# Idle products, a removed filler and a shorter load of the first values at the start of a fused attention and mixture-of-experts kernel

## The chip, the core and the metric

The kernel runs on one core of a Trainium2 chip. A core has a matrix engine (TensorE, "PE" in the profile, with its weight loads as "PEld"), three engines for elementwise work (VectorE "DVE", ScalarE "ACT", GpSimd "POOL"), an engine that issues transfers (SyncE "SP") and sixteen DMA engines that all queues share. Data is in DRAM, in the on-chip memory SBUF, or in PSUM, eight banks into which TensorE writes. The metric is the device time of one execution in microseconds.

## The reference

Eight batches of eight heads, 576 positions, 64 numbers a head, and 32 "packed" queries a head. Two attentions follow each other, then a mixture of experts with one expert a row:

```
def sm_attn(qq, kk, vv):
    s = scale * np.matmul(qq, kk.transpose(0, 1, 3, 2))
    s = s - np.max(s, axis=-1, keepdims=True)
    a = np.exp(s)
    a = a / (np.sum(a, axis=-1, keepdims=True) + 1e-09)
    return np.matmul(a, vv)
p_packed = sm_attn(p, k, v)
out = sm_attn(q, p_packed, p_packed)
...
logits = x @ w_gate
e_idx = np.argmax(logits, axis=1)
...
h = np.maximum(x[mask] @ w1[e], 0.0)
ye = h @ w2[e]
out[mask] = gate_w[mask, None] * eom[mask, e, None] * ye
```

`x` is `out` with the heads side by side: 4608 rows of 512 numbers; `w1[e]` is 512 x 1024 and `w2[e]` is 1024 x 512. Everything is float32.

## The kernel before

The work goes batch by batch. For a batch, `encode` computes the first attention: scores of the packed queries `pt` against the keys (`scores`, `by_head`), maximum, exponential, nine transposes of the weights, the product with the values `vt` (`ps_pp`), a scaling to `ppc`, and its transpose `ppT`. From a sum over `ppT` it guesses the batch's expert (`guess`), whose weights `weights` then loads by a register (`w1`, then `w2` through the staging tiles `wst`). `route` computes the second attention's weights (`ps_s2T`, softmax, `a2T`, `ah`, `al`), `values_up` multiplies the packed values with the expert's first layer (`ps_G`), and `ffn` does the rest (`ps_h`, `hT`, `ps_o`). Rows of other experts are left to a small pass and a loop at the end.

The keys and queries arrive transposed, the values as five blocks of 128 positions: 576 positions are four and a half blocks, and the host fills the half block with zeros. For even heads (`g` = 0) the last block's upper 64 partitions are zero, for odd heads (`g` = 1) its lower 64.

Batch 0 is different, since nothing can hide it. Its keys come in two parts of 320 and 256 positions (`PARTS`), and `packed_by_parts` handles them one behind the other: on TensorE the scores of part one, an idle run `keep_warm(5)`, the scores of part two, then the transposes (`turn`, line 257), five for part one and four for part two, then the product with the values. VectorE and ScalarE work between them.

The order of the work is written out by hand. The string `START` lists the pieces up to the first batch's `ffn`: `k`, `v`, `q` load the next block of keys, values or queries (`fetch`, line 184), `Y` goes one step further in `encode` of batch 0 and `y` in that of the next batch, `t` in `route`, `W` in `weights`, `G` in `values_up`, and a digit calls `keep_warm` with it. Each engine does its instructions in this order. `keep_warm(i)` (line 113) issues products of zeros whose result nobody reads: `CFG["warm"][i]` wide bf16 ones with 512 columns, for `i` = 0 before them `CFG["short"]` small ones, for `i` = 1 an fp32 one with 128 columns instead. `START` as it stands first loads keys and values of batch 0 and then, still before any step of `encode`, its queries and the keys and packed queries of batch 1.

Transfers go through SP's queue and, for three of the first ones, through ScalarE's. Each transfer is given one of eight completion counters in turn (`DMAHW0` to `DMAHW7`), and it is issued only when the transfer that had this counter before has landed.

Of the kernel before, what the change touches and what calls it, by code (L numbers as in the profile page):

```python
# [18 lines left out]

P = 128  # L20
BANK = 512
CFG = dict(raw=6, rq=2, pa=4, w1=2, wst=4, w2=6, a1T=2, at=2, row=2, ht=4, ob=4, up="faaf", last=(4, 2, 3), short=32, warm=(2, 1, 0, 2, 1, 1, 2, 2, 4),
           pool=("w1.0", "w1.1", "w1.2", "w1.3", "w2.0", "w2.1", "w2.2", "w2.3", "w3.3", "w4.3", "w5.3", "w6.3", "w7.3",
                 "al0.0.0"))

START = "kkvvqqkkYYY1YYY3Y4YYtYWttttttyYYt6G7GttGtWtvvqqkkvv"
BESIDE = "8:ry 9:yrr 10:yrrrt 11:yr 12:wrr 13:wrqq 14:rkk 15:r "  # L30
REST = "16:xr 17:x 18:r 19:xvv 20:x 22:x 24:x 25:xxw 26:ww 27:w 28:r 30:r 31:rxxgx 32:xg 33:gw 34:ww"
PLANS = ["1:GG 3:GG 4:GG 5:W 6:W 7:WW 8:W 9:tt 10:tWW 11:Wyy 12:yy 13:tt 14:tt 15:yytt 16:tyy 17:ty 19:y 20:y 21:ryyr 22:yyr "
# [9 lines left out]
def tile_packed_attn_then_moe(ctx, tc, qT, kT, v, pT, w_go, w1, w2, kp, out):  # L42


    nc = tc.nc
# [7 lines left out]
    TF = S // P  # L53
    SF = TF * P
    REM = S - SF
# [9 lines left out]

    NA = CFG["pa"]

# [45 lines left out]
    def keep_warm(i):  # L113

        ps = bank("warm", "a" if i == 5 else "f")
        if i == 0:
            for _ in range(CFG["short"]):
                nc.tensor.matmul(ps[:MQ, :MQ], idle[:, :MQ], idle[:, :MQ], start=True, stop=True)
        for _ in range(CFG["warm"][i]):
            if i == 1:  # L120
# [22 lines left out]
    no_row = float(2 * B * S)  # L143
    key_i = sb.tile([P, B * T * Q * E], I32, tag="hT", name="key_i", bufs=CFG["ht"], **WIDE)
    nc.gpsimd.iota(key_i, pattern=[[1, B * T * Q * E]], base=int(big_id), channel_multiplier=0)
# [11 lines left out]
    row = const.tile([P, B, T], F32, name="row")  # L157
# [16 lines left out]
    def eng(what, *at):  # L174
        return nc.gpsimd if what + ".".join(map(str, at)) in CFG["pool"] else nc.vector

# [7 lines left out]
    def fetch(x):  # L184

        queue = queues["kvq".index(x)]
        if not queue:
            return
        x, b, g = key = queue.pop(0)
        tag = "rq" if x == "q" else "raw"  # L190
        bufs = CFG[tag]
        if x == "v":
            t = sb.tile([P, T, NPAIR * D], F32, tag=tag, name="vt", bufs=bufs, **EVEN)
            (nc.scalar if b == 0 and g else nc.sync).dma_start(t, v[b, g])
        else:
            src = (kT if x == "k" else qT)[b, g]
            if b == 0 and x == "k":
                flat = kT[b].rearrange("h p c s -> (h p c s)")
                at = P * NPAIR * PARTS[0]
                src = (flat[at:] if g else flat[:at]).rearrange("(p c s) -> p c s", c=NPAIR, s=PARTS[g])  # L200
            step = NPAIR // 2 if b == 0 else NPAIR
            if key == ("k", 0, 0):
                n = step * PARTS[0]
                both = sb.tile([P, n + NPAIR * NP], F32, tag=tag, name="kp", bufs=bufs, **EVEN)
                nc.sync.dma_start(both, kp)
                rest = sb.tile([P, step, PARTS[0]], F32, tag="wst", name="k", bufs=CFG["wst"], **EVEN)
                nc.scalar.dma_start(rest, src[:, step:])
                loaded["p", b, g] = both[:, n:].rearrange("p (c n) -> p c n", n=NP)
                loaded[key] = [both[:, c * PARTS[0]:(c + 1) * PARTS[0]] for c in range(step)] + [rest[:, c] for c in range(step)]
                return  # L210
            t = sb.tile([P, NPAIR, src.shape[2]], F32, tag=tag, name=x, bufs=bufs, **EVEN)
            for c in range(0, NPAIR, step):
                (nc.scalar if b == 0 and x == "k" and c else nc.sync).dma_start(t[:, c:c + step], src[:, c:c + step])
            if x == "k" and g == 0:
                pt = sb.tile([P, NPAIR, NP], F32, tag="pt", name="pt", bufs=2)
                nc.sync.dma_start(pt, pT[b])
                loaded["p", b, g] = pt
        if key == ("v", 0, 1):
            nc.sync.dma_start(wgo, w_go)
        loaded[key] = t  # L220
# [704 lines left out]
    def place(plan, b):  # L925

        kinds = dict(x=(encode, 2), y=(encode, 1), Y=(encode, 0), r=(route, 1), t=(route, 0), u=(route, -1), w=(weights, 1), W=(weights, 0),
                     g=(values_up, 1), G=(values_up, 0), l=(first_leftover, 0))
        for c in plan:
            if c in kinds:  # L930
                piece(kinds[c][0], b + kinds[c][1])
            elif c == "d":
                store()
            elif c.isdigit():
                keep_warm(int(c))
            else:
                fetch(c)

    by_hand = tc.manual_schedule()
    by_hand.__enter__()  # L940
    place(START[:4], 0)
    nc.scalar.activation(first, blank[:, 0:1], AF.Exp)
    place(START[4:], 0)
    for b in range(B):
# [74 lines left out]
```

## Time and profile before

| | |
|---|---|
| median of 3 runs | 397.39 us (397.05 to 398.21) |
| the profiled execution | 397.26 us, its span 395.7 us |
| TensorE busy | 387.2 us, 98% of the span |
| VectorE, ScalarE, GpSimd busy | 281.3, 182.2 and 38.3 us |
| DMA | 83.59 MB, mean 211 GB/s |

The profile records one execution. The span runs from its first to its last instruction; the execution's own time is 1.56 us longer. Times in the rows are counted from the span's start. A busy share is an average over stages with different limits, so a stretch is read by what its last wait is for. "releaser" is the instruction or transfer whose end let another one start.

### The profile page before, as it was taken

What the parts mean: (1) busy time and instruction counts of PE and PEld (TensorE: products, weight loads), DVE (VectorE), ACT (ScalarE), POOL (GpSimd) and SP (SyncE); (2) the same over time, 40 slices, a digit from 0 to 9 for tenths busy, and PEclk for the clock granted to TensorE, in tenths of its full rate; (3) what the DMA queues carried; (4) which work ended last, traced back from release to release, by engine and by line L of the source; (5) the groups of instructions that cost most, each with busy time, mean ns of one, the idle gap of its engine ahead of it and who ended that gap; (6) DMA issues with size and microseconds to landing.
All of it is one profiled execution on the core that took longest, in us unless ns stands there. A gap on an engine that the chain in (4) does not pass through costs nothing.

```text
span 395.7 us, 9528 instructions
## 1 busy us (share of the span) xinstructions
PE 387.2 (98%) x3663; PEld 315.4 (80%) x3663; DVE 281.3 (71%) x798; ACT 182.2 (46%) x407; POOL 38.3 (10%) x40
## 2 busy tenths in 40 slices
PE   6999999999999999999999999999999999999995
PEld 3478886879779898787979888788887889798984
DVE  3789699688965977478755886659774796848820
ACT  4375537825545354533726237442645345541401
POOL 3000003510153000200002000020002000020010
PEclk9999999999999999999999999999999999999999
DMA  8999359918961399205990099602961059105901
GB/s 292 338 365 418 117 182 413 391 41 297 406 233 38 117 362 414 80 27 196 402 373 29 16 311 408 240 28 102 348 229 36 28 178 368 40 29 169 322 15 53
DMA packets 36541, 83.59 MB, mean 211 GB/s; under 512 B 3598, under 2 KB 16144, under 8 KB 36496
## 3 DMA queue, kind: packets, MB, share of 16 engines
q1 hardware_dynamic: 36032, 81.74, 56.2%
q10 hardware_dynamic: 432, 1.25, 0.8%
q8 instruction: 29, 0.48, 0.5%
q14 instruction: 16, 0.13, 0.1%
q0 software_dynamic: 32, 0.00, 0.0%
HBM read 67.76 MB, written 15.27 MB: 210 GB/s over the span
## 4 chain that ended last, share of the span: by engine, by line
PE 95%; DMA 4%; SPq 0%; DVE 0%; ACT 0%; issue 0%
PE ps_o L712 45%; PE ps_h L85 26%; PE ps_o L734 8%; PE ps_G L92 4%; PE ps_pp L92 2%; PE ps_s L92 2%; PE ps_s2T L92 2%; DMA vt<-in_v_dram 2%; DMA pt<-in_pT_dram 2%; PE ps_a1T L340 2%; PE ps_lg L92 1%; PE ps_h L662 1%; PE warm L124 1%; PE ps_lo L840 0%; PE ps_lh L840 0%; PE ps_ppT L375 0%
## 5 line engine op out<-in xcount | busy, mean ns | idle before, releaser
L712 PE MATMUL ps_o<-w2h,hT 128*128 128x512 f32 x512 | 165.2, 395 | 0.0
L712 PEld LDWEIGHTS ps_o<-w2h,hT 128*128 128x128 f32 x512 | 96.4, 188 | 23.0 <-issue 1.3
L712 PE MATMUL ps_o<-w2l,hT 128*128 128x512 f32 x256 | 99.9, 390 | 0.0
L681 DVE SCALAR_TENSOR_TENSOR hT<-ps_h,hT 128x256 fp32r<-128x256 f32 x192 | 60.8, 351 | 48.8 <-ACT hT L678 48.0
L85 PE MATMUL ps_h<-ah,Gh 128*128 128x320 f32 (+1 forms) x252 | 76.5, 304 | 0.0
L85 PE MATMUL ps_h<-ah,Gl 128*128 128x320 f32 (+1 forms) x252 | 74.6, 296 | 0.0
L85 PE MATMUL ps_h<-al,Gh 128*128 128x320 f32 (+1 forms) x252 | 74.5, 296 | 0.0
L678 ACT ACTIVATE hT<-ps_h 128x320 fp32r<-128x320 f32 (+1 forms) x128 | 51.5, 414 | 41.1 <-PE ps_h L85 38.8
L597 POOL TENSOR_TENSOR w2l<-wst,w2h 128x1024 fp32r<-128x1024 f32 x13 | 31.8, 2445 | 296.3 <-ACT w2h L594 266.0
L712 PEld LDWEIGHTS ps_o<-w2l,hT 128*128 128x128 f32 x256 | 48.1, 188 | 9.1
L85 PEld LDWEIGHTS ps_h<-ah,Gh 128*128 128x128 f32 x252 | 47.8, 190 | 3.3 <-issue 0.9
L85 PEld LDWEIGHTS ps_h<-al,Gh 128*128 128x128 f32 x252 | 47.8, 190 | 0.4
L85 PEld LDWEIGHTS ps_h<-ah,Gl 128*128 128x128 f32 x252 | 47.8, 190 | 0.0
L594 ACT CAST w2h<-wst 128x1024 fp32r<-128x1024 f32 (+1 forms) x33 | 33.4, 1054 | 0.6 <-PE ps_o L712 0.6
L698 ACT ACTIVATE ob<-ps_o,scm_all 128x512 f32<-128x512 f32 x27 | 18.6, 688 | 31.9 <-PE ps_o L712 27.3
L466 ACT ACTIVATE s<-s 128x576 f32<-128x576 f32 (+2 forms) x18 | 11.4, 633 | 34.3 <-DVE s L463 34.3
L597 DVE TENSOR_TENSOR w2l<-wst,w2h 128x1024 fp32r<-128x1024 f32 (+1 forms) x20 | 23.4, 1168 | 4.9 <-ACT w2h L594 4.8
L77 DVE TENSOR_TENSOR Gl<-ps_G,Gh 128x512 fp32r<-128x512 f32 x28 | 17.4, 682 | 12.9 <-ACT Gh L76 12.9
L734 PE MATMUL ps_o<-w2h,hT 128*128 128x512 f32 x64 | 25.7, 401 | 0.0
L734 PE MATMUL ps_o<-w2l,hT 128*128 128x512 f32 x64 | 25.0, 391 | 0.0
L486 ACT CAST ah<-a2T 128x576 fp32r<-128x576 f32 (+2 forms) x17 | 10.7, 638 | 26.5 <-DVE a2T L478 26.5
L92 PE MATMUL ps_G<-w,ppT 64*32 64x512 f32 (+1 forms) x288 | 16.4, 550 | 0.0
(219 smaller groups left out, 429.2 us busy)
## 6 DMA issues: line engine op xcount, KB each, us to landing
w<-in_w_dram SPq DMA_DIRECT2D x36, 512.0 KB, 5.1
wst<-in_w_dram SPq DMA_DIRECT2D x36, 512.0 KB, 8.6
vt<-in_v_dram SPq DMA_DIRECT2D x15, 640.0 KB, 9.0
k<-in_kT_dram SPq DMA_DIRECT2D x14, 576.0 KB, 10.0
q<-in_qT_dram SPq DMA_DIRECT2D x14, 576.0 KB, 10.4
out_dram<-ob SPq DMA_DIRECT2D x31, 256.0 KB, 3.7
a_d<-a2T SPq DMA_DIRECT2D x16, 320.0 KB, 7.8
q<-in_qT_dram SPq DMA_DIRECT2D x4, 288.0 KB, 6.1
```

The source lines that it names most:

```text
L77: (lo_eng or nc.vector).tensor_tensor(lo, src, f(hi), ALU.subtract)
L85: res = nc.tensor.matmul(dst, a, m, start=j == 0, stop=j == len(seq) - 1)
L92: res = nc.tensor.matmul(dst, a, m, start=j == 0, stop=j == len(seqs[0]) - 1)
L466: nc.scalar.activation(sf[g], sf[g], AF.Exp, scale=QK)
L486: nc.scalar.copy(ah[:, g, ts], a2T[:, g, ts])
L594: nc.scalar.copy(h, x)
L597: eng("w", b, j).tensor_tensor(l, x, f(h), ALU.subtract)
L678: nc.scalar.activation(hT[:, :n], ps, AF.Relu)
L681: nc.vector.scalar_tensor_tensor(hT[:, d0:d0 + s1 - s0], ps[:, s0:s1], 0.0, f(hT[:, s0:s1]), op0=ALU.max, op1=ALU.subtract)
L698: nc.scalar.activation(ob, ob if b < 2 and t_ < 2 else ps, AF.Copy, scale=sc)
L712: nc.tensor.matmul(ps, a, m, start=fc == i == 0, stop=fc == FC - 1 and i == 2)
L734: nc.tensor.matmul(ps, a, m, start=i == 0, stop=i == len(seq) - 1)
```

## The change

Three numbers of the configuration, one character of `START`, and the load of the first batch's values:

- `short` goes from 32 to 24; `warm[0]` from 2 to 8: the products of zeros at the program's start. `warm[5]` goes from 1 to 2: those between the two parts of the first scores.
- The digit `1` behind the third `Y` is gone: one fp32 idle product among the nine transposes.
- The values of batch 0 are loaded in two transfers for each half of the heads: the four full blocks for all 128 partitions, and the last block for the 64 partitions that are not zero. VectorE fills the other 64 with zeros. Later batches load as before.

```
-CFG = dict(... short=32, warm=(2, 1, 0, 2, 1, 1, 2, 2, 4),
+CFG = dict(... short=24, warm=(8, 1, 0, 2, 1, 2, 2, 2, 4),
...
-START = "kkvvqqkkYYY1YYY3Y4YYtYWttttttyYYt6G7GttGtWtvvqqkkvv"
+START = "kkvvqqkkYYYYYY3Y4YYtYWttttttyYYt6G7GttGtWtvvqqkkvv"
...
-            (nc.scalar if b == 0 and g else nc.sync).dma_start(t, v[b, g])
+            queue = nc.scalar if b == 0 and g else nc.sync
+            if b:
+                queue.dma_start(t, v[b, g])
+            else:
+                full, none = (slice(REM, P), slice(0, REM)) if g else (slice(0, REM), slice(REM, P))
+                nc.vector.memset(t[none, TF], 0.0)
+                queue.dma_start(t[:, :TF], v[b, g][:, :TF])
+                queue.dma_start(t[full, TF], v[b, g][full, TF])
```

How this stands on the engines is seen at two places. The first is SP's queue from the first values on (`kp` and an early key block go before them); `vt` are values, `wgo` the weights of the router, `q` and `k` queries and keys, `pt` the packed queries of batch 1, and the bracket names the counter that a transfer waits for. Before:

```order
L194 DMA vt<-in_v_dram 128x1280
L219 DMA wgo<-in_w_go_dram 128x64
L213 DMA q<-in_qT_dram 128x576
L213 DMA q<-in_qT_dram 128x576 [waits DMAHW0_49]
L213 DMA q<-in_qT_dram 128x576 [waits DMAHW1_49]
L213 DMA q<-in_qT_dram 128x576 [waits DMAHW2_49]
L213 DMA k<-in_kT_dram 128x1152 [waits DMAHW3_49]
L216 DMA pt<-in_pT_dram 128x128 [waits DMAHW4_49]
L213 DMA k<-in_kT_dram 128x1152 [waits DMAHW5_49]
```

The same stretch of SP's queue in the changed kernel, with its own line numbers:

```order
L200 DMA vt<-in_v_dram 128x1024
L201 DMA vt<-in_v_dram 64x256
L226 DMA wgo<-in_w_go_dram 128x64 [waits DMAHW0_49]
L220 DMA q<-in_qT_dram 128x576 [waits DMAHW1_49]
L220 DMA q<-in_qT_dram 128x576 [waits DMAHW2_49]
L220 DMA q<-in_qT_dram 128x576 [waits DMAHW3_49]
L220 DMA q<-in_qT_dram 128x576 [waits DMAHW4_49]
L220 DMA k<-in_kT_dram 128x1152 [waits DMAHW5_49]
L223 DMA pt<-in_pT_dram 128x128 [waits DMAHW6_49]
L220 DMA k<-in_kT_dram 128x1152 [waits DMAHW7_49]
```

The order is the same with one transfer more, and ScalarE's queue has one more too, so from `wgo` on each transfer waits for another counter.

The second place is TensorE around the transposes of batch 0, line 257 (`ps_a1T`), between the scores of part two (`ps_s`) and the products with the values (`ps_pp`). Before:

```order
L92 MATMUL ps_s_196<-k,kp 32x256
L92 MATMUL ps_s_197<-k,kp 32x256
L257 MATMUL ps_a1T<-ident,a_206 128x128 x5
L122 MATMUL warm<-blank 128x128
L257 MATMUL ps_a1T<-ident,a_206 128x128 x4
L92 MATMUL ps_pp<-vt,a1T 32x64 x20
```

The same place in the changed kernel:

```order
L92 MATMUL ps_s_199<-k,kp 32x256
L92 MATMUL ps_s_200<-k,kp 32x256
L264 MATMUL ps_a1T<-ident,a_209 128x128 x9
L92 MATMUL ps_pp<-vt,a1T 32x64 x20
L92 MATMUL ps_pp<-vt,a1r 32x64 x4
```

The idle product of line 122 no longer stands between the transposes. Behind this place TensorE's instructions and their order are the same in both kernels, and so are those of GpSimd; VectorE has the two fills more.

## Rows read from the trace of the kernel before

**Rows 1.** The page: span, TensorE's busy time, shares of the chain by engine

```profile
span 395.7 us, 9528 instructions
PE 387.2 (98%) x3663; PEld 315.4 (80%) x3663; DVE 281.3 (71%) x798; ACT 182.2 (46%) x407; POOL 38.3 (10%) x40
...
PE 95%; DMA 4%; SPq 0%; DVE 0%; ACT 0%; issue 0%
```

**Rows 2.** Chain that ended last, first 17 us: start us, us, what

```profile
1.84 7.63 DMA vt<-in_v_dram
9.48 6.49 DMA pt<-in_pT_dram
...
16.11 0.90 PE ps_s L92 x15
```

**Rows 3.** Timeline of TensorE: start us, us, instruction, count, idle before and releaser

```profile
1.24 1.03 PE L118 MATMUL warm<-blank 128*32 128x32 bf16 x32 [1.24 <-DVE blank L106]
2.21 1.03 PE L124 MATMUL warm<-blank 128*128 128x512 bf16 x2
5.38 0.76 PE L92 MATMUL ps_s<-kp 64*32 64x320 f32 x4 [2.14 <-DVE kp L236]
...
9.33 0.63 PE L122 MATMUL warm<-blank 128*128 128x128 f32 x2
9.75 1.06 PE L257 MATMUL ps_a1T<-ident,a 128*128 128x128 f32 x4
...
14.99 0.38 PE L407 MATMUL ps_cs<-one,ones 1*128 1x1 f32 x2
16.11 0.90 PE L92 MATMUL ps_s<-k,pt 64*32 64x288 f32 x16 [0.73 <-DMA pt<-in_pT_dram]
...
19.14 0.66 PE L92 MATMUL ps_G<-w,ppT 64*32 64x256 f32 x16
```

**Rows 4.** Windows: stretch, length, busy by engine, PEclk, DMA share, GB/s

```profile
7.00:8.00 1.00, 1.00 (x17) 0.23 (x16) 0.68 (x2) 0.69 (x3) 0.00 (x0) 1.00 1.00 420
...
14.00:15.00 1.00, 1.00 (x33) 0.36 (x26) 0.83 (x5) 0.00 (x0) 0.00 (x0) 1.00 0.96 387
15.00:16.00 1.00, 0.37 (x10) 0.28 (x2) 0.96 (x4) 0.59 (x3) 0.00 (x0) 1.00 0.29 84
```

**Rows 5.** Groups by form from 7.1, 8.2, 19.1 and 39.6 us: busy us, mean ns

```profile
L92 PE MATMUL ps_s<-k,kp 64*32 64x256 f32 x16 | 1.1, 630 | 0.0
...
L257 PE MATMUL ps_a1T<-ident,a 128*128 128x128 f32 x5 | 1.3, 432 | 0.0
...
L92 PE MATMUL ps_G<-w,ppT 64*32 64x256 f32 x16 | 0.7, 388 | 0.0
...
L340 PE MATMUL ps_a1T<-ident,a 128*128 128x128 f32 x8 | 1.0, 272 | 0.0
```

**Rows 6.** DMA issues at 0.92, 9.86 and 15.12 us: KB, us to landing

```profile
k<-in_kT_dram ACTq DMA_DIRECT2D x1, 320.0 KB, 4.4
...
k<-in_kT_dram SPq DMA_DIRECT2D x1, 576.0 KB, 7.4
...
w<-in_w_dram SPq DMA_DIRECT2D x1, 512.0 KB, 3.5
```

**Rows 7.** Instruction queue from 13.5 to 13.7 us, and whole run: packets, MB, share

```profile
q8 instruction: 1, 0.02, 30.8%
...
q8 instruction: 29, 0.48, 0.5%
```

**Rows 8.** SP's longest wait for values; timeline of SP, VectorE and ScalarE

```profile
SPq L216 <- DMA vt<-in_v_dram: 1.6, 1, 1.6
...
1.84 0.44 SPq L194 DMA_DIRECT2D vt<-in_v_dram  x1
5.09 0.23 DVE L236 TENSOR_SCALAR kp<-kp 128x128 f32<-128x128 f32 x1 [2.88 <-DMA kp<-in_kp_dram]
7.31 0.53 ACT L250 ACTIVATE a<-ps_s,nm 128x320 f32<-128x320 f32 x1 [2.33 <-DVE nm L253]
```

More of the change, by code (lines that the diff above doesn't have):

```diff
@@ L21 @@
 BANK = 512
-CFG = dict(raw=6, rq=2, pa=4, w1=2, wst=4, w2=6, a1T=2, at=2, row=2, ht=4, ob=4, up="faaf", last=(4, 2, 3), short=32, warm=(2, 1, 0, 2, 1, 1, 2, 2, 4),
+CFG = dict(raw=6, rq=2, pa=4, w1=2, wst=4, w2=6, a1T=2, at=2, row=2, ht=4, ob=4, up="faaf", last=(4, 2, 3), short=24, warm=(8, 1, 0, 2, 1, 2, 2, 2, 4),
            pool=("w1.0", "w1.1", "w1.2", "w1.3", "w2.0", "w2.1", "w2.2", "w2.3", "w3.3", "w4.3", "w5.3", "w6.3", "w7.3",
                  "al0.0.0"))
-START = "kkvvqqkkYYY1YYY3Y4YYtYWttttttyYYt6G7GttGtWtvvqqkkvv"
+START = "kkvvqqkkYYYYYY3Y4YYtYWttttttyYYt6G7GttGtWtvvqqkkvv"
 BESIDE = "8:ry 9:yrr 10:yrrrt 11:yr 12:wrr 13:wrqq 14:rkk 15:r "
```

## The prediction

> **What bounds the kernel now.** I read the page's totals first, then the chain of waits, and then only the first 20 us, because every edit lies there. TensorE is busy 387.2 us of a span of 395.7 us and is 95% of the chain that ended last; the DMA has 4% [rows 1]. That 4% is one piece: the chain starts with the first batch's values (issued 1.84, landed 9.47), goes on with the load of the second batch's packed queries, `pt` (issued 9.48, landed 15.97), and from 16.11 to the end it is TensorE [rows 2]. So whatever moves the start of the second batch's scores at 16.11 moves the end one for one, and whatever only makes TensorE reach that place sooner buys idle time in front of it.
>
> The timeline of TensorE shows that place [rows 3]. After idle products that end at 3.24 it has nothing until the first scores at 5.38. It then works through batch 0 up to the small product of line 407 (14.99, last one over at 15.37), and then stands 0.73 us until `pt` lands. Only at 16.11 do the second batch's scores start.
>
> TensorE is slow until about 11 us. [...] It had been idle for 2.1 us just before 5.38 and nearly without a break at work before the rise.
>
> Why does `pt`, 64 KB, take 6.49 us to land? Because SP's queue serves in order, and `pt` stands behind nine earlier transfers on it. The second half of the second batch's keys, next in that queue, was issued at 9.86 and took 7.4 us [rows 6]: it landed at 17.26. The DMA engines move 387 GB/s in 14 to 15 us but only 84 GB/s in 15 to 16, at a share of 0.29 [rows 4]. So most of the sixteen engines had run dry about a microsecond before `pt` had landed: a late remnant held it. At 13.6 us one packet of the instruction queue q8, 0.02 MB, passes on the same engines; the run has 29 of these, 0.48 MB [rows 7]. I take that packet for the cause of the late remnant.
>
> **The change, part by part.**
>
> *Idle products before the first keys* (8 short ones fewer, 6 wide ones more). The 32 short ones last from 1.24 to about 2.21, 0.030 us each; two wide ones end 1.03 us after 2.21, so a slow one follows the other by about 0.43 us [rows 3]. Now 24 short ones end at about 1.96 and 8 wide ones at 1.96 + 8 x 0.43 = 5.4 us, against a first score at 5.38. Nothing is lost in front of the keys, or at most 0.2 us. What it gives is an earlier rise of the clock.
>
> *Between the two parts of the first scores* stands one wide idle product more (0.43 us slow, less than half of that fast), *among the nine transposes* the fp32 idle product goes, which takes the time from 9.33 to 9.75 [rows 3], 0.42 us.
>
> With a fast clock from before 7 us the road to line 407 shortens as follows. Sixteen scores of part two: 1.1 us busy against 0.7 for a group of the same shape [rows 5], 0.45 saved, and everything on VectorE and ScalarE behind them moves up by as much. The last four transposes, 1.06 us for four against 1.0 us for eight [rows 3, 5]: 0.5 saved. The products with the values: about 0.15 by estimate, since they turn fast half way. Sum 1.1 us; the removed idle product lies beside a wait for ScalarE's exponentials, so I do not add it. Line 407 would be over at 15.37 - 1.1 = 14.3 us.
>
> *None of these 1.1 us reaches the end unless `pt` comes sooner too.* It is late next, and its wait then grows from 0.73 to about 1.6 us.
>
> *The values without their zero rows.* Each of the two loads drops 64 KB, 131 kB in all. At the 420 GB/s of 7 to 8 us [rows 4] that is 0.31 us less in front of `pt`. No row shows how fast rows of 1 KB move (half a tile's partitions now get one such row, in a transfer of its own). The bounds are 0 (the 64 small rows take as long as the bytes they replace) and 0.31. I take 0.25, near the upper end, because q and k, with shorter rows than the values, are moved at about the same rate in 14 to 15 us, 387 GB/s.
>
> [...]
>
> *Two more transfers on SP's and ScalarE's queues.* Each costs an issue of about 0.45 us (0.44 for the values on SP) [rows 8]. On ScalarE it pushes the table load and the conversion of the keys; ScalarE then stands 2.33 us before its first exponential, which hides it. The two fills of zeros on VectorE lie in its 2.88 us before the scaling of the packed queries [rows 8]. Without that cover each would cost its own length. On SP a transfer waits for the landing of the one eight places earlier, and two more places shift who waits for whom: the router's weights no longer go at once but when an early key block has landed (0.92 + 4.4 = 5.3 us [rows 6]), the last query block waits for values instead of keys, and `pt` is released by ScalarE's values instead of SP's. Before, `pt` waited 1.6 us there [rows 8]. Now the last query block and the second batch's keys are issued after the values at about 9.2, and `pt` at about 10.1 instead of 9.48. I cost this at nothing, because the queue holds more than 800 KB then, 2 us of work at 0.42 MB per us, and the DMA is busy without a break to 15 us. If that cover were gone, it would cost the 0.6 us by which `pt` is issued later.
>
> *Weights of the first layer.* Their first block is issued at 15.12 and lands 3.5 us later, at 18.6 [rows 6]; its product starts at 19.14 [rows 3]. Issued at about 14.0 it lands no later than now, so it does not bound.
>
> Sum: the second batch's scores start 0.25 us sooner, at 15.86, and TensorE's road to the end is unchanged. The profiled execution took 397.26 us (span 395.7, 1.56 outside), 0.13 under the median of the runs, 397.39. Forecast: 397.26 - 0.25 = **397.0 us**. The clock's phase and small waits behind 16 us may shift it: its own range is 396.5 to 397.5.
>
> **Rivals.**
>
> *A. The late remnant goes away.* If `pt` landed with the rest of its queue, what follows it, 576 KB, would still need 1.4 us up to the emptying at 15.1, so `pt` would have been moved by 13.7 and landed around 14, before TensorE is ready for it at 14.3. Then the whole 1.1 us reach the end: 397.26 - 1.1 = 396.2. For it: TensorE's instruction packet comes at another moment of the queue. Against it: TensorE gets to the same instruction earlier, not later, so the packet still goes before `pt`, and an engine that has to carry it is as late afterwards. [...]
>
> *B. The clock falls back.* TensorE now waits about 1.6 us before the second batch's scores instead of 0.73. [...] Two groups of scores and a group of line 92's G products would cost about 0.45 more each [rows 5], eight wide idle products 8 x 0.2 = 1.6: together 3.0 us, **400.0 us**, slower. For it: before 5.38 there was a gap of 2.1 us and the work after it was slow [rows 3]. Against it: that clock had not been fast before, and the 0.73 us gap left it fast (388 ns afterwards). [...]
>
> *C. `pt` needs its 6.49 us from its issue.* Issued 0.6 us later, it lands 0.6 later: 397.26 + 0.6 = 397.9. For it: the chain names its issue. Against it: the transfer's time is that of a queue in front of it.
>
> **How the numbers follow.** Forecast 0.62, A 0.16, C 0.13, B 0.07, 0.02 for none of these. No change here means within 0.3% of 397.39, that is 396.2 to 398.6, about what a measurement can tell. Faster: more than half of A and a little of the forecast, 0.12. Slower: B and a trace of C, 0.08. The rest 0.80. The range reaches to A's time and over C's: 396.1 to 398.0; it leaves out B and a part of A.
>
> **What would show it.** Right: products of 64x256 at about 390 ns at 7 us, line 407 over by 14.5, a wait for `pt` of 1.3 to 2 us, and scores of batch 1 at 15.7 to 16.0. The first step is wrong if those products still take 630 ns. The second is wrong if `pt` lands before 15 (A) or after 16.3 (C). B shows as products of 600 ns after 16 us. The forecast falls if the scores of batch 1 start sooner by more than 0.8 us or the road behind 16 us changes its length.

## The result, and the profile after

The changed kernel took 399.74 us (median of 5 runs, 398.42 to 400.05) against 397.25 for the kernel before on the same chip: ratio 1.0053, 95% interval 1.0042 to 1.0065. It is slower, by about 2.1 us by the ratio and 2.5 by the two medians; the forecast was 397.0 in a range up to 398.0. Run once more beside other kernels it took 398.85 against 397.34, ratio 1.0042 (1.0028 to 1.0056).

The page of the changed kernel, its span, TensorE's busy time and the chain by engine, against [rows 1]:

```profile
span 398.2 us, 9526 instructions
...
PE 389.5 (98%) x3660; PEld 314.8 (79%) x3660; DVE 281.9 (71%) x800; ACT 182.3 (46%) x407; POOL 38.2 (10%) x40
...
PE 95%; DMA 3%; ACTq 0%; SPq 0%; DVE 0%; issue 0%; ACT 0%
```

2.5 us more of span, and TensorE busy 2.3 us longer with three products fewer. That sum does not locate the loss: the wide idle products at the start alone take 3.59 us instead of 1.03, in time in which TensorE stood before. The timeline of TensorE shows where, to be laid beside [rows 3]:

```profile
1.99 3.59 PE L124 MATMUL warm<-blank 128*128 128x512 bf16 x8
5.75 0.71 PE L92 MATMUL ps_s<-kp 64*32 64x320 f32 x4 [0.16 <-DVE kp L243]
...
14.09 0.38 PE L414 MATMUL ps_cs<-one,ones 1*128 1x1 f32 x2
16.30 1.08 PE L92 MATMUL ps_s<-k,pt 64*32 64x288 f32 x16 [1.83 <-DMA pt<-in_pT_dram]
17.30 1.89 PE L124 MATMUL warm<-blank 128*128 128x512 bf16 x4
...
20.71 0.66 PE L92 MATMUL ps_G<-w,ppT 64*32 64x256 f32 x16
```

Line 407 (now 414) is over at 14.47 instead of 15.37, the wait for `pt` has grown from 0.73 to 1.83, and the second batch's scores start at 16.30 instead of 16.11. Up to here it is the forecast, short of 0.4 us. Behind it four wide idle products take 1.89 us and the first G product starts at 20.71 instead of 19.14. The by-form group at 7.2 us and the windows (stretch, length, busy by engine, PEclk, DMA share, GB/s) say what the clock did, against [rows 4, 5]:

```profile
L92 PE MATMUL ps_s<-k,kp 64*32 64x256 f32 x16 | 0.7, 388 | 0.0
```

```profile
15.00:16.00 1.00, 0.00 (x0) 0.00 (x0) 0.96 (x3) 0.76 (x4) 0.00 (x0) 1.00 1.13 317
16.00:17.00 1.00, 0.70 (x16) 0.21 (x16) 0.84 (x3) 0.42 (x1) 0.00 (x0) 0.76 0.98 225
17.00:18.00 1.00, 1.00 (x10) 0.28 (x3) 0.86 (x4) 0.54 (x2) 0.00 (x0) 0.50 0.73 270
...
20.00:21.00 1.00, 1.00 (x41) 0.43 (x26) 0.00 (x0) 0.53 (x3) 0.00 (x0) 1.00 1.03 414
```

The 64x256 products take 388 ns at 7 us instead of 630: TensorE is fast that early, at a granted clock (PEclk) that reads 1.00 from 7 to 8 us in both kernels. Then, behind the wait for `pt`, the granted clock falls to 0.50, where it stays until about 20 us, and the 64x288 products take 598 and 622 ns, 412 and 415 before. That is rival B, and it was my first theory of the loss. It did not hold: of the five runs, one had a mean granted clock of 1.000, so no such fall, and took 399.52 us.

Where the 2.5 us of this trace lie: 1.57 up to the first G product, 0.32 from there to the last output's issue (394.42 against 392.53), and 0.6 behind that issue, where no work is left. Nearly all of the 0.32 comes at one place: around 234 us ScalarE starts an activation 0.28 us later behind the same product, and everything behind it is late by as much. ScalarE in the kernel before, then in the changed one:

```profile
233.98 0.44 ACT L678 ACTIVATE hT<-ps_h 128x320 fp32r<-128x320 f32 x1 [0.85 <-PE ps_h L85]
```

```profile
235.83 0.98 ACT L685 ACTIVATE hT<-ps_h 128x320 fp32r<-128x320 f32 x2 [1.13 <-PE ps_h L85]
```

All eight traces of kernels with one transfer more on ScalarE's queue show the wait of 1.12 to 1.14, the ten others 0.85 to 0.87. Why is not shown.

The chain, against [rows 2], goes the same way as before, from the values to `pt`, and then to TensorE:

```profile
1.85 7.74 DMA vt<-in_v_dram
...
10.46 5.70 DMA pt<-in_pT_dram
16.16 0.14 issue
16.30 1.08 PE ps_s L92 x16
17.37 1.82 PE warm L124 x4
```

It passes over SP's queue, and that is where the change sits. SP's waits up to 17 us (waited for, us, times, longest), against [rows 8], and its timeline (start us, us, issues):

```profile
SPq L226 <- DMA k<-in_kT_dram: 2.6, 1, 2.6
SPq L220 <- DMA vt<-in_v_dram: 1.8, 1, 1.8
```

```profile
2.32 0.74 SPq L201 DMA_DIRECT2D vt<-in_v_dram  x1
5.62 0.33 SPq L226 DMA_DIRECT2D wgo<-in_w_go_dram  x1
6.00 3.94 SPq L220 DMA_DIRECT2D q<-in_qT_dram  x4
9.98 0.43 SPq L220 DMA_DIRECT2D k<-in_kT_dram  x1
10.46 0.43 SPq L223 DMA_DIRECT2D pt<-in_pT_dram  x1
```

Before, the four query blocks went from 3.08 to 7.38 and the keys at 7.42. Now the router's weights wait 2.6 us for a key block, the last query block 1.8 for values; it is through at 9.94, and the keys follow. The first weights, issued at 14.22 (KB, us to landing, against [rows 6]):

```profile
w<-in_w_dram SPq DMA_DIRECT2D x1, 512.0 KB, 5.5
```

### The profile page after: what moved, and what is told of

The parts are those of the page before. It is cut to its first block, busy times and chain, and to the rows that moved or that the text cites. A ratio compares the mean times of both kernels' runs of the same rounds, so it can differ in the third digit from the quotient of the medians.

```text
span 398.2 us, 9526 instructions
## 1 busy us (share of the span) xinstructions
PE 389.5 (98%) x3660; PEld 314.8 (79%) x3660; DVE 281.9 (71%) x800; ACT 182.3 (46%) x407; POOL 38.2 (10%) x40
## 4 chain that ended last, share of the span: by engine, by line
PE 95%; DMA 3%; ACTq 0%; SPq 0%; DVE 0%; issue 0%; ACT 0%
PE ps_o L719 45%; PE ps_h L85 26%; PE ps_o L741 7%; PE ps_G L92 4%; PE ps_s L92 2%; PE ps_pp L92 2%; DMA vt<-in_v_dram 2%; PE ps_s2T L92 2%; PE ps_a1T L347 2%; DMA pt<-in_pT_dram 1%; PE ps_lg L92 1%; PE warm L124 1%; PE ps_h L669 1%; PE ps_lh L847 0%; PE ps_lo L847 0%; PE ps_ppT L382 0%
## 5 line engine op out<-in xcount | busy, mean ns | idle before, releaser
L705 ACT ACTIVATE ob<-ps_o,scm_all 128x512 f32<-128x512 f32 x27 | 18.6, 688 | 31.7 <-PE ps_o L719 27.2
```

The lines of the kernel that those rows point to most:

```text
L705: nc.scalar.activation(ob, ob if b < 2 and t_ < 2 else ps, AF.Copy, scale=sc)
```

## The experiments

Each was timed in five rounds beside the kernel before (397.25 to 397.85 in different sittings); the ratio to it counts.

**The split load alone** (the edit of `fetch` put into the kernel before).

> The kernel before with the split load of the first batch's values alone (two more transfers). Theory T (the clock falls in the long wait for pt, about 1.4 us; the two extra transfers lengthen the end of the program by 0.6): TensorE reaches line 407 no sooner than before, its wait for pt is about 0.9, no fall; the second batch's scores start 0.2 later at 16.3, the end of the program grows by 0.6: 397.3 + 0.8 = 398.1. Rival R (the extra transfers themselves cause the loss, the slow products are only a sign of late data): 399.5 or more, with slow products after 16 us. Rival N (the longer end is unrelated to the transfers): 397.5.

1.0055 (1.0028 to 1.0082), 2.2 us slower, the whole loss and no fall of the clock: PEclk is 1.00 throughout. The timeline of TensorE:

```profile
15.93 0.99 PE L92 MATMUL ps_s<-k,pt 64*32 64x288 f32 x16 [0.65 <-DMA pt<-in_pT_dram]
...
20.90 0.67 PE L92 MATMUL ps_G<-w,ppT 64*32 64x256 f32 x16 [1.78 <-DMA w<-in_w_dram]
```

`pt` is even earlier than before; what is late is the first weights, 5.7 us from issue to landing against 3.5 [rows 6]. Theory T is wrong for this kernel; R's time is met, without the slow products that it named.

**The idle edits alone** (the changed kernel with the old load of the values).

> The kernel before with the edits of the idle products alone, the values loaded as before. Theory T: pt lands at about 16.0 as before, line 407 is over about 1 us sooner, the wait of 1.6 to 1.8 makes the clock fall, products of 64x256 take about 600 ns after 16 us, 1.4 us lost there and nothing at the program's end: 398.7. Rival R: no slow products, 397.3. Rival N: the end of the program is longer here as well, 399.3.

0.9979 (0.9970 to 0.9988), 0.8 us faster. TensorE:

```profile
14.61 0.72 PE L92 MATMUL ps_s<-k,pt 64*32 64x288 f32 x16 [0.31 <-DMA pt<-in_pT_dram]
...
18.30 0.67 PE L92 MATMUL ps_G<-w,ppT 64*32 64x256 f32 x16 [0.22 <-DMA w<-in_w_dram]
```

In this trace `pt` has landed by 14.6 and the weights, asked for 1.07 us sooner (14.05), land at 18.2. Theory T is wrong here too: no long wait and no fall. The two halves of the change multiply to 0.9979 x 1.0055 = 1.0034, and 1.0053 and 1.0042 were measured for both: the loss needs nothing more than the split load.

**The gap filled** (eight wide idle products between line 414 and the scores of batch 1).

```
-START = "...YYtYWttttttyYYt6G7..."    warm=(8, 1, 0, ...)
+START = "...YYtYWtttttt2yYYt6G7..."   warm=(8, 1, 8, ...)
...
-ps = bank("warm", "a" if i == 5 else "f")
+ps = bank("warm", "a" if i in (2, 5) else "f")
```

> The changed kernel with eight wide idle products between line 414 and the second batch's scores (8 x 0.22 = 1.75 us of the 1.83 it waited for pt). Theory T: TensorE hardly stands, the granted clock stays 1.00, the scores start at 16.2 to 16.3 as in the changed kernel, line 669 comes 1.4 sooner; the longer end stays: 399.7 - 1.4 = 398.3. Rival R: the products after 16 us stay slow or late, 399.7. If eight are too many: the scores start later than 16.4 and 398.5 comes out.

1.0033 (1.0020 to 1.0046); the clock stays at 1.00, the scores start at 16.76 although `pt` landed at 15.6: too many products here, and 1.3 us of loss are left without any fall. The first weights were in time in this trace (14.14 + 4.2 = 18.3); the loss is made of 0.47 at the first G product, which follows the late scores (19.61), 0.34 behind it and 0.6 at the end.

**As many transfers as before** (queries of batch 0 whole, in the changed kernel).

```
-step = NPAIR // 2 if b == 0 else NPAIR
+step = NPAIR // 2 if b == 0 and x == "k" else NPAIR
```

> The changed kernel with the first batch's queries in one transfer for each half instead of two, so that the program has as many transfers as before the change. Theory T: the wait for pt and the fall stay about as they are, but the end of the program is 0.6 shorter: 399.1, the time from the last output's issue to the end of the span back from 3.7 us to 3.1. Rival N: the end stays 3.7, 399.7. Rival R (the number of transfers decides the whole loss): 397.5.

0.9981 (0.9967 to 0.9995): this one edit gives back nearly everything, the start and the end; theory R. In the same sitting the median is 397.18, that of the idle edits alone 396.88, and the 0.28 us around 234 us are still in its trace. `pt` was waited for 1.21 us, and the clock did not fall.

**The packet of the instruction queue** (60 instructions fewer in front: `short=0`, `warm[0]=4` in the kernel before).

> The kernel before with the 32 short idle products in front replaced by two wide ones: the same time on TensorE, 60 instructions fewer. Theory F (the 16 KB packet of TensorE's instruction queue, at 13.60 in the kernel before, holds one DMA engine back, and pt with it): the packet passes after 15 us, pt lands at 14.1 to 14.6 on all engines instead of 15.97, TensorE does not wait for it behind line 407 (over at 15.4), the scores of batch 1 start at 15.4 to 15.6: 397.8 - 0.6 = 397.2, or 397.5 if the first weights, landing at 18.6, take most of it back. Rival L (the late engine has nothing to do with that packet): pt lands at 16.0 as before, 397.8.

1.0002 (0.9992 to 1.0011). TensorE:

```profile
14.84 0.72 PE L92 MATMUL ps_s<-k,pt 64*32 64x288 f32 x16
...
18.55 0.67 PE L92 MATMUL ps_G<-w,ppT 64*32 64x256 f32 x16 [0.22 <-DMA w<-in_w_dram]
```

The packet (0.48 MB in 29 of them [rows 7], so 16.6 KB for one) passed at 14.42, later than the 13.60 of the kernel before and not after 15, the scores start 1.27 us sooner with no wait for `pt`, the first G product 0.59, and the time is the same. The 0.59 last until about 70 us: there ScalarE waits for an output tile that is still being stored, 2.27 us instead of 1.55, and starts later than before (69.91 against 69.81):

```profile
69.91 0.69 ACT L698 ACTIVATE ob<-ps_o,scm_all 128x512 f32<-128x512 f32 x1 [2.27 <-DMA out_dram<-ob]
```

So a `pt` that lands on time is worth little. The same edit with 44 instructions, on the idle edits alone:

> The idle edits alone (values whole), with the 24 short idle products replaced by two wide ones, 44 instructions fewer, the same time on TensorE. Theory F: the packet of the instruction queue passes later than the 13.31 of the run with the idle edits alone, pt lands at 14.5 or sooner, and the load of the first weights bounds from 18.2: 396.9 or up to 0.2 less. If the packet now falls among the keys that stand before pt, one engine is late again: pt at 15.5 to 16, 397.5. Rival L: as the idle edits alone, 396.9, whatever the packet does.

0.9991 (0.9982 to 1.0000); the packet passed at 13.38, `pt` was waited for 1.47 us, and the first G product still came at 18.56. With 60 instructions fewer on the split load alone:

> The split load with the 32 short idle products in front replaced by two wide ones, 60 instructions fewer. Theory F (with the keys issued later the packet of the instruction queue gets in front of them): the packet passes after 13.5, pt lands at 14.8 or sooner, the first weights by 19.0; the end stays 0.6 longer: 398.0. Rival: the slow stretch of the DMA between 13 and 15 us (253 to 319 GB/s in the kernels with the split load, 391 to 407 without) comes from the transfers alone: 1.5 to 2.2 over before as with the split load alone.

1.0054 (1.0034 to 1.0074), the loss unchanged, first G product at 20.92. Theory F is ruled out as its cause. Nor does the packet's moment decide when `pt` lands: with two transfers behind `pt` (below) it passed at 13.60, as in the kernel before, and `pt` landed at 14.9 and not at 15.97. None of these three times shows a cost of the packet, against my reading of [rows 4, 7].

**The end of the program** (kernel before, one late output stored in three pieces).

> The kernel before with one output tile of the fifth batch (256 KB, around 240 us) stored in three transfers instead of one: two transfers more, none of them near the start. Theory C (two more transfers shift which completion counter the last transfer has, and the engines wait for the counters one by one at the end): the first 230 us are unchanged, from the last transfer's issue to the end of the span 3.7 us instead of 3.1: 397.8 + 0.6 = 398.4. Rival N (the longer end of the kernels with the split load came from something else): 397.8.

1.0014 (1.0005 to 1.0023). Its timeline of SP, span and last issue, and that of the kernel before:

```profile
core 0 of [0], span 396.5 us
...
392.68 0.33 SPq L723 DMA_DIRECT2D out_dram<-right  x1
```

```profile
core 0 of [0], span 395.7 us
...
392.53 0.33 SPq L721 DMA_DIRECT2D out_dram<-right  x1
```

3.8 us behind the last issue instead of 3.2, and only 0.15 up to it: theory C holds. It is 3.8 in the changed kernel as well. SP's waits for the counters at the end, one behind another, show the mechanism. In the kernel before, three were left when the last transfer had landed (394.24); in the changed kernel (396.13), as here, nine:

```profile
L954 SPq EVENT_SEMAPHORE  x3: 27/28/28, 394.2 to 394.4; - x3
```

```profile
L961 SPq EVENT_SEMAPHORE  x9: 28/28/28, 396.1 to 396.6; - x9
```

The other engines have three and nine of these waits left as well. The last one through, the queue of TensorE's weight loads (51 ns a wait), is at its branch behind them at 394.6 and at 397.1, 0.4 and 1.0 us after the landing: the 0.6.

The first 230 us of this program are those of the kernel before, so it gives a second trace of them. Here `pt` landed at 14.8 instead of 15.97, TensorE did not wait for it, and the first G product came no sooner (19.27 against 19.14):

```profile
15.51 0.70 PE L92 MATMUL ps_s<-k,pt 64*32 64x288 f32 x13
...
19.27 0.66 PE L92 MATMUL ps_G<-w,ppT 64*32 64x256 f32 x16
```

The late `pt` of [rows 2] belongs to that one execution.

**The changed kernel again.**

> The changed kernel once more, unchanged, for a second trace of it. Theory T (the fall of the clock is what it loses after 16 us): the granted clock falls again between 16 and 20, products of 64x256 take about 600 ns. Theory W (the loss is a late landing of pt or of the first weights, and the fall only one form of it): clock 1.00 throughout and the same 399.7, with the first G product at 20.5 or later because it waits for its weights.

The clock stayed at 1.00 in this trace, behind a wait of 1.43 us, and the kernel was still slower (1.0042). TensorE:

```profile
15.78 0.72 PE L92 MATMUL ps_s<-k,pt 64*32 64x288 f32 x16 [1.43 <-DMA pt<-in_pT_dram]
...
19.67 0.67 PE L92 MATMUL ps_G<-w,ppT 64*32 64x256 f32 x16 [0.97 <-DMA w<-in_w_dram]
```

The scores start at 15.78, sooner than before, and the weights are late: theory W, if at 19.67 and not at 20.5. In the first trace, too, the weights landed only at 19.7 (14.22 + 5.5), so the fall cost there about 1.0 us, from 19.7 to 20.71, and not the 1.4 that I had charged to it.

**Two useless transfers of 32 bytes** in the place of the split.

```
+if x == "v" and b == 0:
+    tiny = const.tile([1, 8], F32, name=f"tiny{g}")
+    (nc.scalar if g else nc.sync).dma_start(tiny, v[b, g][:1, TF, :8])
```

> The kernel before, values loaded whole, with two more transfers of 32 bytes each that nothing uses, one behind the values on SP's queue and one on ScalarE's, where the split load has its own. Theory O (the order: two more transfers make SP issue the last query block, the keys and pt later, at 9.6 to 10.5 instead of 7.0 to 9.5): the start is lost as with the split load alone, the first weights land at 19.5 or later, plus 0.6 at the end: 1.0 to 2.0 over before, 398.6 to 399.5. Theory S (the shape: rows of 1 KB on half the partitions): the start is that of before, only the end is longer: 0.6 over before, 398.1.

1.0063 (1.0043 to 1.0083), as much as the split load. Neither the bytes nor the rows of 1 KB are needed for the loss; two more transfers at these places are enough. SP's timeline and the window from 11 to 15 us:

```profile
6.39 3.95 SPq L213 DMA_DIRECT2D q<-in_qT_dram  x4
10.43 0.39 SPq L213 DMA_DIRECT2D k<-in_kT_dram  x1
```

```profile
11.00:15.00 4.00, 3.71 (x127) 2.34 (x126) 2.21 (x12) 0.64 (x2) 0.42 (x2) 1.00 0.94 299
```

The kernel before moves 412 GB/s there:

```profile
11.00:15.00 4.00, 3.84 (x127) 2.28 (x119) 1.97 (x11) 0.49 (x2) 0.00 (x0) 1.00 1.04 412
```

**The split load with whole queries, without the idle edits.**

> The split load alone with the first batch's queries in one transfer for each half: as many transfers as before the change, and SP issues the keys at about 7.6 again. Theory O: neither the start nor the end loses, within 0.3 of before, and the DMA engines move 380 to 400 GB/s from 13 to 15 us. Theory S: the start loses 1.0 to 1.5 as in the run with the split load alone, 398.5 or more.

1.0006 (0.9998 to 1.0015). Theory O holds, and no gain from the saved 131 kB can be seen. Two more transfers of the values, one of them on ScalarE's queue, with an early last query block therefore lose nothing at the start. Its profiled run was far from the median (400.83 against 397.88): SP took 3.46 us for the four issues of the first weights, 1.94 in the kernel before, and they landed late. Only the DMA's rate before that, 400 GB/s, and the clock (below) are used of it.

**Which issue counts.** One tiny transfer, on SP alone:

> The kernel before with one transfer of 32 bytes more on SP's queue behind the values, none on ScalarE's. SP issues the query blocks as before (the last at about 7.3), the keys only when the values have landed (9.5 instead of 7.4), pt at about 10. Theory K (the late issue of the keys loses the time): the DMA engines move under 330 GB/s from 13 to 15 us, the first weights land at 19.5 or later, 1.0 to 1.6 over before. Theory Q (the late last query block is needed too): as before, within 0.3. The end of the program is not longer: the last transfer has the next counter but one.

1.0012 (1.0003 to 1.0020). Keys and `pt` go nearly as late as in the changed kernel (9.60 against 9.98 and 9.71), the last query block 1.4 us sooner or more, and the rate stays:

```profile
5.72 2.52 SPq L213 DMA_DIRECT2D q<-in_qT_dram  x4
9.60 0.33 SPq L213 DMA_DIRECT2D k<-in_kT_dram  x1
10.07 0.33 SPq L216 DMA_DIRECT2D pt<-in_pT_dram  x1
```

```profile
11.00:15.00 4.00, 3.83 (x127) 2.27 (x119) 2.33 (x13) 0.58 (x2) 0.23 (x1) 1.00 1.04 403
```

Theory K falls; the ratio is a loss of 0.5 us all the same, more than theory Q's 0.3. Two behind `pt` and the keys:

> The kernel before with two transfers of 32 bytes more on SP's queue behind pt and the second batch's keys. Nothing in front of them is issued later, the counters at the end are shifted by two. Theory O (order in front of the keys): the start is as before, the end 0.6 longer: 0.5 to 0.7 over before. Rival (any two transfers more near the start desynchronise the engines): 1.5 to 2.3 over before, as with two in front.

1.0021 (1.0012 to 1.0029): the end alone, since the last output is issued at 392.39, before the 392.53 of the kernel before. Two between the last query block and the keys:

> The kernel before with two transfers of 32 bytes more on SP's queue between the last query block and the second batch's keys. SP issues the last query block as before (7.0 to 7.8), the keys, pt and the second half of the keys as late as with the split load or later (9.9 to 11.2). Theory Q (the cover: with the last query block already queued 3 us of work cover the later issues): DMA rate 390 or more from 11 to 14 us, first weights by 18.7, only the end 0.6 longer: 0.5 to 0.8 over before. Rival P (two transfers anywhere in front of pt): 305 to 320 GB/s, first weights at 19.5 or later, 1.5 to 2.5 over before.

1.0037 (1.0013 to 1.0060), a wide interval because of one run at 401.5; the median is 0.8 over before. SP's timeline and the window:

```profile
3.23 3.55 SPq L217 DMA_DIRECT2D q<-in_qT_dram  x4
10.06 0.36 SPq L217 DMA_DIRECT2D k<-in_kT_dram  x1
```

```profile
11.00:15.00 4.00, 3.72 (x116) 2.16 (x104) 2.31 (x12) 0.34 (x2) 0.13 (x1) 1.00 1.05 397
```

Keys later than in the changed kernel, the first weights at 18.6, and nothing lost at the start, as theory Q had it. Over the kernels that have a trace (end of the last query block's issue, from SP's timeline, and rate from 11 to 15 us, from the windows):

| last query block issued by | kernels | GB/s, 11 to 15 us |
|---|---|---|
| 6.2 to 8.2 us | the twelve others: before, both kernels of the idle edits, all with whole queries, tiny transfers elsewhere or one alone, two late pieces, `pt` behind the keys, fewer instructions | 397 to 416 |
| 9.7 to 10.0 | changed (twice), gap filled | 346 to 365 |
| 10.3 to 10.5 | split alone, two tiny, split with fewer instructions | 299 to 316 |

A late last query block and a low rate go together in all eighteen traces. Every kernel with a late block also has a transfer more on ScalarE's queue; that transfer alone is not the cause, since the two kernels with it and with whole queries keep 403 and 400 GB/s, but a late block without it was not run.

**A long wait at the fast clock** (idle edits alone, `pt` loaded behind the second half of the keys).

> The idle edits alone (values whole), with pt loaded behind the second half of the second batch's keys instead of in front of it: TensorE, fast since about 6 us, waits for pt from 14.2 to about 16.9, 2.6 us. Theory B (a long enough wait drops the clock): the granted clock falls to 0.5 during or behind this wait in every run, products of 64x256 take about 600 ns, first G product at 21 or later: 399.5. Rival: it stays at 1.00 as in the waits of 1.43 to 1.78 us that left it fast; scores at 16.9, first G product 3.1 later at 20.0: 398.2.

1.0055 (1.0042 to 1.0068). In the trace the clock stayed at 1.00 although the wait was longer than the one it fell behind:

```profile
17.03 0.72 PE L92 MATMUL ps_s<-k,pt 64*32 64x288 f32 x16 [2.48 <-DMA pt<-in_pT_dram]
```

That run took 398.05 at a mean granted clock of 0.998. The four others took 399.5 to 400.7 at 0.990 to 0.994, 1.4 us or more longer. They have no trace, so that their clock fell behind this wait is likely and not shown. A second fall is on record in the disturbed run of the split load with whole queries: 2.32 us of waiting for the first weights up to 21.19, then the clock at half (window 23 to 24 us):

```profile
23.00:24.00 1.00, 1.00 (x16) 0.54 (x18) 1.00 (x4) 0.00 (x0) 0.00 (x0) 0.50 0.67 172
```

The split load with fewer instructions waited 2.17 us and kept it. What decides it in a single run is open.

**Sooner still** (idle edits alone, whole queries, one late output in three pieces).

> The idle edits alone (values whole) with the first batch's queries in one transfer for each half, so SP issues keys and pt two places sooner (about 6 to 7.5 us), and one late output stored in three transfers, so that the counters at the end are those of before. Theory O: keys and pt are on time, pt at 14.5 or sooner, the first weights at 18.2; the gain over before that the idle edits alone had (0.97) stays or grows by up to 0.3: 0.9 to 1.3 under before. Rival (earlier issue gains nothing, larger query transfers delay the scores that need them): 0.5 to 1.0 under before.

0.9986 (0.9975 to 0.9997): no more gain than with the idle edits alone, which remain the best of both kernels' parts, 0.9979. In its trace the first G product came 0.81 us sooner than before, as there (0.84), and at the wait for an output store around 70 us about 0.3 of it was gone.

## Why the prediction was wrong

*Idle products: right.* 390 ns at 7 us were forecast, 388 measured; line 407 over by 14.5 forecast, 14.47 measured. The first scores started at 5.75 and 5.52 in the two traces, so up to 0.37 later where at most 0.2 was allowed. The wait for `pt` was put at 1.6 and came out at 1.43 and 1.83. The sum of 1.1 us takes the slow products up to 11 us for a lower clock. No run shows that: the granted clock reads 1.00 there, and what the traces show is the durations, 630 ns at 7 us before and 388 in the changed kernel.

*"None of these 1.1 us reaches the end unless `pt` comes sooner too": misleading.* The idle edits alone gave 0.8 us. In both their traces `pt` did land sooner, at about 14.5 with a wait of 0.31 us and at about 15.6 with one of 1.47 (the run with 44 instructions fewer), but the gain was not set by it: a `pt` sooner by 1.1 us than in the other trace brought the first G product only 0.26 further (18.30 against 18.56). What these edits bring forward is the guess of batch 0's expert, and with it the issue of the first weights, from 15.12 to 14.05. I had looked at these weights and written that they do not bound, since 18.6 lies before 19.14. Half a microsecond of slack is no slack when the edits move things by one.

*"Whatever moves the start of the second batch's scores at 16.11 moves the end one for one": wrong.* Scores 1.27 us sooner brought the first G product 0.59 sooner and the end nothing, and in the trace with the two late pieces scores 0.6 sooner brought not even the G product forward. The chain of waits names the wait that ended last in one execution. The weights stood close behind it, and at 70 us ScalarE's wait for an output store.

*"Two more transfers on SP's and ScalarE's queues ... I cost this at nothing": this is the step that failed.* The term was about 2.2 us (the split load alone, 1.0055); in the trace of that run 1.76 lie in front of the first G product, 0.3 around 234 us and 0.6 at the end. The working had the right facts: the last query block, keys and `pt` issued late, and 2 us of work left in the queue. It took 2 us for cover enough, and, for the case without cover, priced only `pt`, at 0.6. Measured: with the last query block issued at 9.7 or later the DMA moves 299 to 365 GB/s from 11 to 15 us instead of some 400, and the first weights land at 19.5 to 20.9 instead of 18.6 (at 18.3 in the kernel with the gap filled alone). With this block out by 8.2 us the same late keys cost nothing at the start; that the work then queued is the cover is my reading of it, and no row shows the queue's length. "The DMA is busy without a break to 15 us" held by the share (1.01 from 11 to 15 us in the changed kernel) and not by the bytes (357 GB/s there, 412 before). The weights' landing is stretched (5.5 us instead of 3.5). No row shows single DMA engines: the windows give the mean of all sixteen, and a nearly full share with fewer bytes (0.94 and 299 GB/s with the two tiny transfers, 1.04 and 412 before) means that they were busy longer for each byte. Why a later issue makes them so, and whether one engine lags, is not shown.

*The end of the program and ScalarE's 0.28 us around 234 us were not in the sum at all.* The end costs 0.6 us, by the two late pieces and by every kernel with two transfers more.

*Values, 0.25 us: not seen.* They landed at 9.59 instead of 9.47, and the time with restored order (1.0006) shows no gain. Since that run also pays the 0.28 us around 234 us, its interval does not rule out 0.25.

*Rivals.* A happened in the run with the idle edits alone: `pt` on time, but the gain was the weights'. It happened in a trace of the unchanged start as well, with no gain. C: `pt` took 5.70 us from its later issue and came 0.19 later, not 0.6. B was seen in one of the two traces. It was priced at 3.0 us and cost 1.0 to 1.4 there; it was put at 400.0, and the median was 399.74. That agreement is chance, since the split load alone, without a fall, takes as long.

What stays open: why a late last query block lowers the rate and how that turns into late weights (with the gap filled the rate was 346 GB/s and the weights were in time), and when a wait of 1.4 to 2.5 us drops the clock.

## What to carry to other kernels

A transfer added to a queue whose issues wait for earlier landings is not priced by its bytes (two of 32 bytes cost 2.5 us here): write down, for each later issue, which landing it will now wait for, and how much work the queue then holds; restoring the count (here by joining two other transfers, 0.9981 instead of 1.0053) is cheaper than any of it. Beside the wait that the chain names, look for every landing within a microsecond of it, because an edit that moves one uncovers the next (here the first weights, in at 18.6 for a product at 19.14). A busy DMA share is no proof of flow: read the GB/s beside it (0.94 and 299 GB/s with the two tiny transfers, 1.04 and 412 before).

## What the runs showed that I had not expected

Two 32-byte transfers that nothing reads cost 2.5 us. Two more transfers, at each of the places tried, lengthen the end of the program by 0.6 us, and one more does not (3.1 us behind the last issue). One more on ScalarE's queue near the start delays an activation at 234 us by 0.28 (a wait of 1.13 us instead of 0.85). The same binary had its granted clock fall to 0.50 behind a wait of 1.83 us in one trace and keep it behind 1.43 in the next, while other kernels kept it behind 2.17 and 2.48.
